# Sixteen-way stores, value loads in two transfers, and the first batch's values summed on VectorE, in a fused attention and expert kernel

## The chip, the cores and the metric

The kernel runs on one core of a Trainium2 chip. The core has TensorE (PE, matrix multiply; its weight loads are listed as PEld), VectorE (DVE), ScalarE (ACT), GpSimd (POOL) and SyncE (SP). DMA moves data between DRAM and the on-chip memory SBUF; here POOL issues the loads, SP and, in the last batch, ACT issue the stores. Matmul results go to a second memory, PSUM, which VectorE and ScalarE read. The metric is the device time of one execution in microseconds (us).

## The reference

Eight batches, eight heads, 576 rows, head size 64. Keys and values are averaged over groups of 8 rows (72 groups), and the attention output of all heads, 4608 rows of 512, goes to a top-1 router over eight experts. Cut to what matters:

```python
k_p = k.reshape(B, H, 72, 8, D).mean(axis=3);  v_p = v.reshape(B, H, 72, 8, D).mean(axis=3)
attn = softmax(q @ k_p.T / sqrt(D));           x = attn @ v_p          # to (4608, 512)
logits = normalize(x) @ normalize(expert_emb).T / tau
e = argmax(logits);  gate = softmax(logits)[e]
out = gate * (relu(x @ w1[e]) @ w2[e])         # w1[e]: 512x1024, w2[e]: 1024x512
```

## The kernel before, in words

The batches are worked on one after another, with the attention of the next batch laid between the expert matmuls of the present one. For each batch the kernel guesses one expert for all of its rows, from the router's logits of the batch's mean row, and loads that expert's weights while the attention still runs. After the last batch it checks the guess; a loop (line 1068, called the repair loop here) would redo rows for other experts. In these data it has nothing to do, but every engine passes its entry, where it waits on the semaphores of everything that is still under way.

**Attention of a batch** (`attention`). POOL loads k, q and v (`load_k`, `load_q`, `load_v`, lines 880 to 900), converting from float32 to float16. v lands as 72 partitions (groups) of 8 heads x 8 rows x 64. VectorE adds key rows in pairs and transposes them (`k0`, `k1`, `kT`), and transposes q in three parts called units (`q0` to `q2`, line 432). For each unit u, TensorE makes scores (line 471), ScalarE takes exp (478), TensorE multiplies by the values (`pv`, 489), VectorE divides by the row sums (`xs`, 499 and 501) and transposes the result into `xt_all` (`x_turn`, 507), which holds x as the later matmuls want it; ScalarE squares it for the norm (`square`, 516). When all three squares are there, `route` (530) makes the logits and the norms.

**Values.** In batches 1 to 7 VectorE adds the eight value rows of a group in three halving steps (`v_add`, 445 and 449), in place, into `vpx`. In batch 0 TensorE sums them as eight matmuls with the identity (`v_sum`, 455), and ScalarE copies the sum into `vpx` (`v_out`, 461). The mean row that the guess needs comes from `vpx` (`mean`, 593), in batch 0 from the raw values (`mean_raw`, 602: 64 matmuls of one column, 8 heads x 8 rows). `guess` (615), `guess_out` with MAX8 (622) and a register load on POOL lead to the issue of the weight loads (319, 324).

**Experts of a batch** (`ffn`). "Hidden" matmuls (`h_part`, 749) make 64 groups of 128 hidden values: two of the eight (w = 0, 1; the argument `early` is 2) in three parts, one for each unit, as soon as that unit's x is there; the other six in halves of 288 columns. ScalarE applies relu (`relu`, 758). "y" matmuls (`y_part`, 769; `y_last`, 798) make four tiles of 128 rows (c = 0 to 3) and one of 64 rows held as two half rows (c = 4). ScalarE or VectorE multiplies by the gate (786, 788, 807) and `store` (877) writes the tile out. The last batch's tile c = 3 is written to `y_end` (780, 782) and stored in two pieces after the repair loop (1113 on SP, 1114 on ACT).

**Rows.** Row i*36 + t of a batch (i of 16, t of 36) stands in column t*16 + i of `xt_all`, so a y tile's partitions are 8 t by 16 i, and a store's outer dimension in DRAM is t: 8 for c < 4, 4 for c = 4 and for each piece of `y_end`.

**What sets the order.** A planner (`Plan`) gives each step an engine, an estimated time, the steps it needs and a priority, tries 400 random shifts of the priorities, and writes the instructions out in the order found. Each engine then runs its list in order and waits on semaphores. Changed estimates or dependencies therefore change the order everywhere. In stretches where the plan has TensorE idle it writes filler matmuls (`warm`, 371), which are fixed in the program. The waits come from the tile framework, which compares which parts of a tile an instruction reads and writes.

Of the kernel before, what the change touches and what calls it, by code (L numbers as in the profile page):

```python
# [242 lines left out]
def kernel(  # L243
# [114 lines left out]


# [26 lines left out]
    def attention(b, early=False):  # L386
# [54 lines left out]
        def v_add(level):  # L441
            vv = loads['v', b].rearrange("g h (r d) -> g h r d", d=D)
            n = POOL >> (level + 1)
            if level < 2:
                nc.vector.tensor_tensor(out=vv[:, :, 0:n], in0=vv[:, :, 0:n],  # L445
                                        in1=vv[:, :, n:2 * n], op=ALU.add)
                return
            new_vpx()
            nc.vector.tensor_tensor(out=st['vpx'][:, :, 0:D], in0=vv[:, :, 0],
                                    in1=vv[:, :, 1], op=ALU.add)  # L450

        def v_sum():
            st['pv'] = psum()
            for r in range(POOL):
                nc.tensor.matmul(out=st['pv'][0:G, 0:H * D], lhsT=ident_h[0:G, 0:G],
                                 rhs=loads['v', b][:, :, ts(r, D)],
                                 start=(r == 0), stop=(r == POOL - 1))

        def v_out():
            new_vpx()  # L460
            nc.scalar.copy(out=st['vpx'][:, :, 0:D],
                           in_=st['pv'][0:G, 0:H * D].rearrange("g (h d) -> g h d", h=H))
# [42 lines left out]
        def x_turn(u):  # L505

            nc.vector.transpose(  # L507
                out=xt_all[:, b].rearrange("p w (t l) -> p t w l", l=32)[:, ts(u, 6)],
                in_=st['x', u].rearrange("p b j d -> p (b j d)").rearrange(
                    "p (t l w) -> p t w l", w=4, l=32))  # L510

        def square(u):
            if 'sq' not in st:
                st['sq'] = xp.tile([128, 4, S], BF16, name="sq", bufs=1)
            cs = ts(u, 192)
            nc.scalar.activation(out=st['sq'][:, :, cs], in_=xt_all[:, b, :, cs],  # L516
                                 func=AF.Square)
# [79 lines left out]
        def mean_raw():  # L597

            pm = st['pm'] = psum()
            for h in range(H):  # L600
                for r in range(POOL):
                    nc.tensor.matmul(out=pm[ts(h % 2, 64), h // 2:h // 2 + 1],
                                     lhsT=loads['v', b][:, h, ts(r, D)], rhs=ones_m[0:G, 0:1],
                                     start=(r == 0), stop=(r == POOL - 1))
# [75 lines left out]
        if early:  # L680
            step('mean', 'PE', 1.5, mean_raw, ['lv', 'const'], -30, tiles=1)
            step('vs', 'PE', 1.75, v_sum, ['lv', 'guess'], -25, tiles=1)
            step('v', 'ACT', 0.5, v_out, ['vs'], -30, frees=[('vs', 0)])
# [20 lines left out]
        for u in range(NU):  # L704
            step(f's{u}', 'PE', 0.53, lambda u=u: score(u),
                 ['kT', f'q{u}', (f'pv{u}', b - 1)], b - 10, tiles=2)
            for p in range(2):
# [6 lines left out]
            step(f'x{u}', 'DVE', 0.92, lambda u=u: x_turn(u), [f'xs{u}'], b - 1.6)  # L714
            step(f'sq{u}', 'ACT', 0.75, lambda u=u: square(u),
                 [f'x{u}', ('route', b - 1)], b - 4)
# [15 lines left out]
    def ffn(plan, b, xt, w, get_gm, finish, last=False, early=0):  # L732
# [9 lines left out]
        def h_part(w, u):  # L742


            n, step_ = (SU, 256) if w < early else (HALF, 512)
            if u == 0:
                st['ph', w] = psum(plan)
            for kk in range(4):
                nc.tensor.matmul(out=st['ph', w][:, ds(u * step_, n)],  # L749
                                 lhsT=w1v[:, kk, w // 4, (w // 2) % 2, w % 2, :],  # L750
                                 rhs=xt()[:, kk, ts(u, n)],
                                 start=(kk == 0), stop=(kk == 3))

        def relu(w):
            n, step_ = (SU, 256) if w < early else (HALF, 512)
            if ('hT', w // 4) not in st:
                st['hT', w // 4] = hp_.tile([128, 2, 2, S], FP16, name=f"hT{w // 4}")
            nc.scalar.activation(  # L758
                out=st['hT', w // 4][:, (w // 2) % 2, w % 2, :].rearrange(
                    "p (r c) -> p r c", c=n),  # L760
                in_=st['ph', w].rearrange("p (r c) -> p r c", c=step_)[:, 0:S // n, 0:n],
                func=AF.Relu)
# [60 lines left out]
        for w, u in order:  # L823
# [3 lines left out]
            hs[w, u] = chain(0.33 if w < early else 0.495, lambda w=w, u=u: h_part(w, u), xs,  # L827
# [13 lines left out]
        for part in parts:  # L841
            if part is None:
                o = chain(0.98, y_last, before('lw2', 'copy') + relus, 1)
                plan.step('ACT', 1.4 if last else 0.85, y_last_out, [o, *gm], -10 + pri,
                          frees=[(o, 0)], store=0.45)
# [5 lines left out]
            if half:  # L851
                o = ys[c if last else c // 2 * 2, 0]
                if last:
                    plan.step('DVE' if c % 2 == 0 else 'ACT', 0.7 if c % 2 == 0 else 1.2,
                              lambda c=c: y_out(c), [ys[c, 1], *gm], -10 + pri,
                              frees=[(o, 0)], store=0.82)
                elif c % 2:
                    for i in (c - 1, c):
                        plan.step('ACT', 0.6, lambda i=i: y_out(i), [ys[i, 1], *gm],
                                  -10 + pri, frees=[(o, 0)] if i == c else [], store=0.82)  # L860
# [3 lines left out]
    def out_rows(o_b, c, y_sb):  # L864

        rows = o_b.rearrange("(i t) d -> t i d", t=T)
        if c < 4:
            return [(rows[ts(c, 8)], y_sb)]
        DH = DM // 2
        return [(rows[32:T, :, ts(j, DH)], y_sb[ts(j, 64), 0:DH]) for j in range(2)]  # L870
# [11 lines left out]
    with tc.manual_schedule():  # L882
# [6 lines left out]
        def load_v(b, after=()):  # L889
            def emit():  # L890
                vv = loads['v', b] = inp.tile([G, H, POOL * D], FP16, name="vv")
                nc.gpsimd.dma_start(out=vv, in_=grouped(v, b))
            done['lv', b] = load(0.9, 3.6, emit, [('v', b - 2), ('vs', b - 2), *after])
# [218 lines left out]
    for dst, src in out_rows(out[ts(B - 1, S)], 3, y_end):  # L1112
        nc.sync.dma_start(out=dst[0:4], in_=src[0:64])
        nc.scalar.dma_start(out=dst[4:8], in_=src[64:128])
# [34 lines left out]
```

The softmax here doesn't subtract the row's maximum and nothing guards it: scores larger than these inputs give would overflow.

## Time and profile before

| | us |
|---|---|
| runs | 219.91, 219.10, 218.87, 215.33 |
| median | 218.99 |
| the profiled execution's own time | 217.82 |
| its span, first to last instruction | 216.1 |
| TensorE busy in the span | 191.1 (88%), of it 17.0 in 58 fillers |
| VectorE, ScalarE, POOL busy | 143.8, 126.4, 35.3 |
| first y matmul of batch 0 | 36.18 |
| compute ends (`y_end` written) | 206.60 |
| last store issued, landed | 211.39, 215.15 |

Busy shares are averages over three stretches that have different limits: the head up to the first y matmul, the middle, and the tail after the last matmul. Busy time of matmuls is modelled from a pipeline; an engine that is busy may still wait a little. Landings are read from the semaphores that a transfer's parts post.

### The profile page before, as it was taken

Reading aid. Unit: us, or ns where it says so; the run is one execution under the profiler, and the core shown is the slowest. Engines: PE = TensorE matmul, PEld = TensorE weight load, DVE = VectorE, ACT = ScalarE, POOL = GpSimd, SP = SyncE. Lnnn points to the kernel's source line nnn. Section 1 sums busy time; section 2 is a strip of 40 time slices with the busy share of each in tenths; the row PEclk is TensorE's granted clock in tenths of the full one; section 3 lists DMA queues with packets and bytes.
Section 4 is the critical chain, followed back from the end, with each engine's and each line's share of the span. In section 5 each row is a group of like instructions: output and inputs, shape, how many; then the busy total and the mean of one; then the engine's idle time right before and its main releaser. Section 6 shows DMA issues by size and latency. Waiting matters only on the chain. (4 is left out here: it accounts for less than half of the span.)

```text
span 216.1 us, 7393 instructions
## 1 busy us (share of the span) xinstructions
PE 191.1 (88%) x3155; PEld 119.9 (56%) x3156; DVE 143.8 (67%) x391; ACT 126.4 (58%) x203; POOL 35.3 (16%) x61
## 2 busy tenths in 40 slices
PE   6879999988987999997998999889998999999900
PEld 2355586455752487455864586448654864586400
DVE  3745968199689836976796869766977895642200
ACT  3037455594693377547766768477857677775300
POOL 7107026003200043003201420132000100020000
PEclk9985699999996999999999999999999999999995
DMA  4998999999997269999984999999955400340231
GB/s 76 192 160 136 207 217 185 208 222 234 251 212 131 46 165 199 208 222 195 243 164 91 194 207 239 212 226 224 239 135 142 167 1 11 92 125 1 55 123 53
DMA packets 18486, 34.63 MB, mean 160 GB/s; under 512 B 2440, under 2 KB 9224, under 8 KB 17936
## 3 DMA queue, kind: packets, MB, share of 16 engines
q0 software_dynamic: 12992, 24.65, 62.3%
q1 hardware_dynamic: 5184, 9.00, 13.0%
q8 instruction: 26, 0.43, 0.8%
q10 hardware_dynamic: 272, 0.46, 0.6%
q14 instruction: 12, 0.10, 0.1%
HBM read 61.88 MB, written 9.44 MB: 330 GB/s over the span
## 5 line engine op out<-in xcount | busy, mean ns | idle before, releaser
L749 PE MATMUL pa<-xt_all,w 128*128 128x288 f16 (+1 forms) x576 | 67.6, 273 | 1.6 <-DVEq L666 0.6
L769 PE MATMUL pa<-w,hT 128*128 128x512 f16 x256 | 62.8, 386 | 4.9 <-ACT y_sb L786 2.8
L749 PEld LDWEIGHTS <-w 128*128 128x128 f16 x576 | 52.3, 98 | 14.7 <-issue 4.2
L758 ACT ACTIVATE hT<-pa 128x576 f16<-128x576 f32 x64 | 40.7, 647 | 17.3 <-PE pa L749 16.5
L478 ACT ACTIVATE at<-pa 72x768 f16<-72x768 f32 x48 | 36.6, 803 | 12.4 <-PE pa L471 12.0
L769 PEld LDWEIGHTS <-hT 128*128 128x128 f16 x256 | 23.4, 98 | 31.4 <-issue 7.5
L786 ACT ACTIVATE y_sb<-pa,gm 128x512 f32<-128x512 f32 x29 | 19.1, 685 | 24.8 <-PE pa L769 24.7
L516 ACT ACTIVATE sq<-xt_all 128x768 bf16<-128x768 f16 x24 | 20.0, 842 | 10.4 <-DVE xt_all L507 10.2
L432 DVE STREAM_TRANSPOSE qT<-qq 128x768 f16<-128x768 f16 x24 | 22.6, 962 | 3.1 <-DMA qq<-in_q_dram 2.9
L501 DVE TENSOR_TENSOR x_sb<-pa,rc 128x768 f16<-128x768 f32 x24 | 23.0, 957 | 0.8
L507 DVE STREAM_TRANSPOSE xt_all<-x_sb 128x768 f16<-128x768 f16 x24 | 22.8, 965 | 0.3
L319 POOL DMA_DIRECT2D w<-in_moe_w_dram x10 | 4.2, 417 | 96.4 <-DMA w<-in_moe_w_dram 40.4
L499 DVE RECIPROCAL rc<-pa 128x12 f32<-128x12 f32 x24 | 5.3, 222 | 21.2 <-PE pa L489 20.7
L547 POOL TENSOR_TENSOR rn<-lgT,half_c 128x5 f32<-128x5 f32 x8 | 9.5, 1190 | 56.5 <-DVE lgT L552 56.5
L371 PE MATMUL pa<-ones_m 128*128 128x512 f16 x58 | 17.0, 437 | 1.7 <-DVE half_c L975 1.7
L489 PEld LDWEIGHTS <-at 72*32 72x32 f16 x1152 | 11.9, 100 | 8.7 <-ACT at L478 4.6
L471 PE MATMUL pa<-qT,kT 32*72 32x192 f16 x384 | 14.3, 257 | 2.4 <-DVE kT L423 0.9
L489 PE MATMUL pa<-vpx,at 72*32 72x65 f16 x1152 | 14.9, 201 | 1.7 <-ACT at L478 1.4
L471 PEld LDWEIGHTS <-kT 32*72 32x72 f16 x384 | 8.5, 111 | 10.8 <-issue 5.5
L445 DVE TENSOR_TENSOR vv<-vv 72x2048 f16<-72x2048 f16 (+1 forms) x14 | 13.1, 935 | 0.2
L552 DVE STREAM_TRANSPOSE lgT<-pa 128x160 f32<-128x160 f32 x8 | 2.8, 349 | 14.5 <-PE pa L530 14.5
L371 PEld LDWEIGHTS <-ones_m 128*128 128x128 f16 x58 | 5.9, 108 | 8.1 <-issue 3.2
(98 smaller groups left out, 151.8 us busy)
## 6 DMA issues: line engine op xcount, KB each, us to landing
w<-in_moe_w_dram POOLq DMA_DIRECT2D x14, 1024.0 KB, 16.3
out_dram<-y_sb SPq DMA_DIRECT2D x30, 256.0 KB
kk<-in_k_dram POOLq DMA_DIRECT2D x8, 576.0 KB, 17.4
vv<-in_v_dram POOLq DMA_DIRECT2D x8, 576.0 KB, 25.3
qq<-in_q_dram POOLq DMA_DIRECT2D x7, 576.0 KB, 17.7
w<-in_moe_w_dram POOLq DMA_DIRECT2D x4, 512.0 KB, 6.5
out_dram<-y_sb SPq DMA_DIRECT2D x15, 64.0 KB
qq<-in_q_dram POOLq DMA_DIRECT2D x1, 384.0 KB
```

The lines of the kernel that those rows point to most:

```text
L371: nc.tensor.matmul(out=pa[:, 0:512], lhsT=ones_m[:, 0:128], rhs=ones_m[:, 0:512], start=True, stop=True)
L432: nc.vector.transpose(out=qT.rearrange("p w r (t i) -> p t w r i", i=16), in_=qq.rearrange("p t (w r i) -> p t w r i", w=2, r=2))
L471: nc.tensor.matmul(out=pS[a // 2][0:G, ds(a % 2 * 512 + r * SU, SU)], lhsT=kT[ts(a, 32), w, r, :], rhs=qT[ts(a, 32), w, r, :], start=(w == ...
L478: nc.scalar.activation(out=at.rearrange("g a r c -> g a (r c)"), func=AF.Exp, scale=escale, in_=st['pS', u][p][0:G].rearrange("g (a c) -> ...
L489: nc.tensor.matmul(out=px[ts(a, 32), c0:c0 + D + 1], lhsT=st['at', u, a // 2][:, a % 2, r, ts(j, 32)], rhs=st['vpx'][:, 2 * a + r, 0:D + 1 ...
L501: nc.vector.tensor_tensor(out=x_sb, in0=pxv[:, :, :, 0:D], in1=rc.unsqueeze(3).to_broadcast([128, 2, 6, D]), op=ALU.mult)
L507: nc.vector.transpose(out=xt_all[:, b].rearrange("p w (t l) -> p t w l", l=32)[:, ts(u, 6)], in_=st['x', u].rearrange("p b j d -> p (b j d ...
L516: nc.scalar.activation(out=st['sq'][:, :, cs], in_=xt_all[:, b, :, cs], func=AF.Square)
L749: nc.tensor.matmul(out=st['ph', w][:, ds(u * step_, n)], lhsT=w1v[:, kk, w // 4, (w // 2) % 2, w % 2, :], rhs=xt()[:, kk, ts(u, n)], start ...
L758: nc.scalar.activation(out=st['hT', w // 4][:, (w // 2) % 2, w % 2, :].rearrange("p (r c) -> p r c", c=n), in_=st['ph', w].rearrange("p (r ...
L769: nc.tensor.matmul(out=py, lhsT=st['hT', w // 4][:, (w // 2) % 2, w % 2, ts(c, 128)], rhs=w2[:, w // 2, w % 2, :], start=(w == 0), stop=(w ...
L786: nc.scalar.activation(out=y_sb, in_=py, func=AF.Copy, scale=g)
```

## The change

- **Stores.** The columns of `xt_all` are laid out so that a y tile's partitions are 16 i by 8 t (c = 4: 16 i by 4 t), and a store's outer dimension in DRAM is 16. For this the transpose of a unit writes single columns 8 apart (4 apart in the last 64 columns) and is made in two pieces of four and two blocks of 32, since a unit's six blocks fall into two column tiles. `y_end` is stored in two column halves instead of two row halves.
- **Units of columns.** Finished columns after units 0, 1 and 2 are now 0 to 128, to 384 and to 576; the squares and the hidden matmuls of w = 0, 1 go by these thirds (`third`). The square of a unit is declared to need all transposes up to its own.
- **Value loads.** Each goes in two transfers, of 64 and of 8 partitions.
- **Batch 0's values.** `v_sum` and `v_out` go; `v_add` sums on VectorE, into a tile of the pool that later holds hidden values, since `mean_raw` still reads the raw values. `mean_raw` takes heads in pairs, whose outputs lie in different halves of the columns.
- **The planner** gets other estimates for transposes, squares, hidden parts, value loads and stores.

```diff
+    def third(u):
+        return slice((0, 128, 384)[u], (128, 384, S)[u])
...
         def v_add(level):
             vv = loads['v', b].rearrange("g h (r d) -> g h r d", d=D)
             n = POOL >> (level + 1)
+            to = vv
+            if early:
+                if level == 0:
+                    half = hp_.tile([128, 2, 2, S], FP16, name="hT0")
+                    st['half'] = half[0:G].rearrange("g a r s -> g (a r s)")[
+                        :, 0:H * 4 * D].rearrange("g (h r d) -> g h r d", h=H, d=D)
+                to = st['half']
+                if level > 0:
+                    vv = to
             if level < 2:
-                nc.vector.tensor_tensor(out=vv[:, :, 0:n], in0=vv[:, :, 0:n],
+                nc.vector.tensor_tensor(out=to[:, :, 0:n], in0=vv[:, :, 0:n],
...
         def x_turn(u):
-            nc.vector.transpose(
-                out=xt_all[:, b].rearrange("p w (t l) -> p t w l", l=32)[:, ts(u, 6)],
-                in_=st['x', u].rearrange("p b j d -> p (b j d)").rearrange(
-                    "p (t l w) -> p t w l", w=4, l=32))
+            src = st['x', u].rearrange("p b j d -> p (b j d)").rearrange(
+                "p (m s i w) -> p m w s i", w=4, s=2, i=16)
+            m = 0
+            for c, n in ((0, 4), (1, 2), (1, 2), (2, 4), (3, 4), (4, 2))[2 * u:2 * u + 2]:
+                m0 = 2 if (c, u) == (1, 1) else 0
+                nc.vector.transpose(
+                    out=xt_all[:, b, :, cols(c)].rearrange(
+                        "p w (i m s) -> p m w s i", i=16, s=2)[:, m0:m0 + n],
+                    in_=src[:, m:m + n])
+                m += n
         def square(u):
-            cs = ts(u, 192)
+            cs = third(u)
...
         def mean_raw():
-            for h in range(H):
+            for h in range(0, H, 2):
                 for r in range(POOL):
-                    nc.tensor.matmul(out=pm[ts(h % 2, 64), h // 2:h // 2 + 1],
-                                     lhsT=loads['v', b][:, h, ts(r, D)], rhs=ones_m[0:G, 0:1],
+                    for i in range(2):
+                        nc.tensor.matmul(out=pm[ts(i, 64), h // 2:h // 2 + 1],
+                                         lhsT=loads['v', b][:, h + i, ts(r, D)],
...
         if early:
             step('mean', 'PE', 1.5, mean_raw, ['lv', 'const'], -30, tiles=1)
-            step('vs', 'PE', 1.75, v_sum, ['lv', 'guess'], -25, tiles=1)
-            step('v', 'ACT', 0.5, v_out, ['vs'], -30, frees=[('vs', 0)])
+            step('v0', 'DVE', 0.85, lambda: v_add(0), ['lv'], -25)
+            step('v', 'DVE', 0.9, lambda: [v_add(1), v_add(2)], ['v0'], -25)
...
-            step(f'x{u}', 'DVE', 0.92, lambda u=u: x_turn(u), [f'xs{u}'], b - 1.6)
-            step(f'sq{u}', 'ACT', 0.75, lambda u=u: square(u),
-                 [f'x{u}', ('route', b - 1)], b - 4)
+            step(f'x{u}', 'DVE', 0.98, lambda u=u: x_turn(u), [f'xs{u}'], b - 1.6)
+            step(f'sq{u}', 'ACT', (0.54, 0.96, 0.75)[u], lambda u=u: square(u),
+                 [*(f'x{i}' for i in range(u + 1)), ('route', b - 1)], b - 4)
...
         def h_part(w, u):
-            n, step_ = (SU, 256) if w < early else (HALF, 512)
+            cs = third(u) if w < early else slice(u * HALF, u * HALF + HALF)
+            to = cs.start + 128 if w < early else u * 512
...
     def out_rows(o_b, c, y_sb):
-        rows = o_b.rearrange("(i t) d -> t i d", t=T)
+        rows = o_b.rearrange("(i t) d -> i t d", t=T)
         if c < 4:
-            return [(rows[ts(c, 8)], y_sb)]
+            return [(rows[:, ts(c, 8)], y_sb)]
         DH = DM // 2
-        return [(rows[32:T, :, ts(j, DH)], y_sb[ts(j, 64), 0:DH]) for j in range(2)]
+        return [(rows[:, 32:T, ts(j, DH)], y_sb[ts(j, 64), 0:DH]) for j in range(2)]
...
                 vv = loads['v', b] = inp.tile([G, H, POOL * D], FP16, name="vv")
-                nc.gpsimd.dma_start(out=vv, in_=grouped(v, b))
-            done['lv', b] = load(0.9, 3.6, emit, [('v', b - 2), ('vs', b - 2), *after])
+                for gs in (slice(0, 64), slice(64, G)):
+                    nc.gpsimd.dma_start(out=vv[gs], in_=grouped(v, b)[gs])
+            done['lv', b] = load(1.4, 3.1, emit, [('v', b - 2), ('mean', b - 2), *after])
...
     for dst, src in out_rows(out[ts(B - 1, S)], 3, y_end):
-        nc.sync.dma_start(out=dst[0:4], in_=src[0:64])
-        nc.scalar.dma_start(out=dst[4:8], in_=src[64:128])
+        for eng, cs in ((nc.sync, slice(0, DM // 2)), (nc.scalar, slice(DM // 2, DM))):
+            eng.dma_start(out=dst[:, :, cs], in_=src[:, cs])
```

## The prediction

> **What bounds the kernel now.** I read the page first, then the waits of TensorE, then the head and the tail as timelines, because the busy shares say that the middle is full and the ends are not.
>
> ```profile
> PE 191.1 (88%) x3155; PEld 119.9 (56%) x3156; DVE 143.8 (67%) x391; ACT 126.4 (58%) x203; POOL 35.3 (16%) x61
> PEclk9985699999996999999999999999999999999995
> ```
>
> TensorE is busy 88% of the span, 17.0 us of it with 58 fillers (L371). The second line is its granted clock in 40 slices of 5.4 us: about half speed in slices 4 and 5, lower in slice 13. Its waits from 24 to 206 us:
>
> ```profile
> PE pa L769 <- ACT y_sb L786: 2.8, 6, 0.7
> PE pa L769 <- issue: 2.1, 2, 1.2
> PE pa L489 <- ACT at L478: 0.9, 3, 0.4
> ```
>
> They are small and scattered, and no load stands among the large ones: in the middle it is TensorE's own work, in the planner's order, that sets the time. The head, in time order (start, duration, then the instruction):
>
> ```profile
> 12.45 1.49 PE L602 MATMUL pa<-ones_m,vv 72*64 72x1 f16 x64 [0.85 <-DMA vv<-in_v_dram]
> 13.91 0.98 DVE L432 STREAM_TRANSPOSE qT<-qq 128x768 f16<-128x768 f16 x1 [2.90 <-DMA qq<-in_q_dram]
> 14.41 2.99 PE L455 MATMUL pa<-vv,ident_h 72*72 72x512 f16 x8
> 17.44 0.58 ACT L461 CAST vpx<-pa 72x512 f16<-72x512 f32 x1 [3.31 <-PE pa L455]
> 22.16 2.74 PE L371 MATMUL pa<-ones_m 128*128 128x512 f16 x6
> 27.07 1.15 PE L749 MATMUL pa<-xt_all,w 128*128 128x192 f16 x12
> 36.18 4.48 PE L769 MATMUL pa<-w,hT 128*128 128x512 f16 x20
> ```
>
> The value sum takes TensorE 2.99 us at half clock (granted 0.50 from 15.07 to 25.3 us), and the first y matmul comes at 36.18. The tail, and DMA from 203 to 216 us in 40 slices of 0.33 us (busy tenths, GB/s):
>
> ```profile
> 206.13 0.47 ACT L782 ACTIVATE y_end<-pa,gm 128x256 f32<-128x256 f32 x1 [2.86 <-DVE y_end L780]
> 210.23 1.07 ACTq L1114 DMA_DIRECT2D out_dram<-y_end  x1
> 211.39 0.59 SPq L1113 DMA_DIRECT2D out_dram<-y_end  x1
> DMA  2552354554457564411000000131222222210000
> GB/s 82 142 66 32 57 158 158 183 176 164 176 202 246 189 208 170 164 69 76 32 0 0 0 0 25 50 57 38 63 101 101 95 76 101 101 69 6 0 0 0
> ```
>
> Compute ends at 206.6; the last stores are issued 3.6 and 4.8 us later. Between lie the repair loop's semaphore waits (L1068). The trace's semaphore events say which binds: SP has passed seven of them by 207.4, passes the c=1 store's at 208.30 and the c=2 store's at 209.89, the moment those stores land. The last store, started at 212.36, lands at 215.15. So **the path's last 9.5 us are stores**.
>
> **Stores on sixteen engines.** How many DMA engines a transfer uses can be counted in the semaphore events: of 16 posts, the engines left out post at once. A c<4 store (outer dimension 8) has eight late posts, a 64 KB store (outer 4) four. After the change the outer dimension is 16 everywhere. Rows for the price: four engines with 16 KB each land 1.4 to 1.6 us after the first post (201.79 to 203.38); eight with 32 KB each, queue empty, 2.5 to 3.4 (189.30 to 192.70); overlapped, 4.2 (c=2, 205.70 to 209.87). With sixteen, c=2 is 16 KB per engine: 1.5 us, landing at 207.2, ahead of the waits SP walks through anyway. SP then passes at 207.6 instead of 209.89: 2.3 us. The end store goes from 32 KB on each of four engines (2.8 us) to 8 KB on each of sixteen: I take 1.5, gaining 1.3. Sum 3.6. Lower bound: sixteen engines together reach no more than the 200 GB/s that eight show above; then c=2's 256 KB take 1.3 us plus the 0.9 that the 64 KB row leaves over (1.6 less 64 KB at half that rate), landing at 207.9, and the end stores' 256 KB take 2.2; the gains are 1.9 and 0.6: 2.5. Upper: the end store in 1.2, so 3.9. I take **3.6**. Earlier stores need no price: no row shows TensorE waiting for one.
>
> **Value loads in two transfers.** The first load shows four posts at 8.12 to 8.38 and twelve at 11.57 to 12.40: twelve engines, six rows each. After: 64 rows are four per engine, the other eight add one on eight engines, so five rows instead of six; 4.3 us from 8.06 becomes 3.6, landing near 11.7 instead of 12.40. POOL issues one more transfer per load; its issue rows (L892 0.87, L899 0.56) put that at about 0.5 us, eight times, under a POOL that is 16% busy. Not shown is an 8-row load; its issue lies between nothing, since it cannot shorten the first one's, and one L892 more.
> The Trainium skill ("DMA: Bandwidth & Descriptors", Rules for kernel authors) advises against two transfers to disjoint partitions, as both spread over the same engines anyway. The same page (Why a DMA increments its semaphore by 16 and not by 1) takes the largest count up to 16 that divides the outer sizes, 12 for 72 rows, and the twelve late posts agree. By the first rule the load gains nothing, by the second 0.7 us; the total moves by neither, as follows.
>
> **Batch 0's values on VectorE.** TensorE loses eight matmuls (2.99) and ScalarE one cast (0.58); VectorE gets three adds. Batch 1's same adds run from 25.18 to 27.53: 2.35 us. They stand ahead of the second q transpose, so 11.75 to 14.1, then q until 15.0, and the expert choice (MAX8, 14.81 before) comes 0.15 later: the first weights are issued at 16.65 instead of 16.50. The raw mean with alternating column tiles is 64 matmuls; bounds are 1.49 (no gain) and 1.2 (the already alternating mean, L593, eight in 0.29); it ends before the adds either way and hides. The mean now precedes the first score (11.07 before, about 13.0 after); its exp ends at 15.0 and nothing waits longer for it than for the second q.
> So P·V no longer waits for 18.02: second score 15.0 to 15.9, P·V 0 to 16.7, two fillers, third score at 17.6, its exps until 20.2, P·V 2 ends at 21.1 instead of 22.2. But the planner puts nine fillers there (six before), fixed in the program: at half clock 9 x 0.427 = 3.85, until 24.9.
>
> **New waits.** The changed kernel's built instructions show what the diff does not: the second transpose piece of unit 1 now waits for unit 0's square, the first piece of unit 2 for unit 1's square and, in batches 0, 1 and 3, for hidden matmuls (L749) of unit 1. Before, transposes waited for VectorE alone. In batch 0, after the fillers, unit 0's eight matmuls end near 25.7, w=0 of unit 1 at 26.2 to 26.6, and only then does the transpose run (0.95): hidden matmuls of unit 2 start at 27.3 to 27.7. Before, at 27.07, 16 remained; now 8. From there: 8 x 0.088 + 48 x 0.1225 + route, mean and guess 1.2 = 7.8, five fillers 1.1: first y matmul at 36.2 to 36.6 against 36.18. **Head: +0.2.** Behind the waiting transpose stand batch 1's value adds (27.3 instead of 25.18), its guess and the next weights' issue (32.84), covered by DMA work queued until 39.8. Clock bounds: full speed again at 21.9 saves 1.9; half speed until 28.7 costs 1.7.
> In the other batches unit 2's scaling (0.23 + 0.96, start to start about 1.2) stands before the wait, and the 4 x 256 square needs about 1.05 (768 elements take 0.84): hidden, 0. Cover gone, about 1 us a batch.
>
> **Two pieces per transpose.** 24 more instructions at 0.06 (0.86 start to start against 0.80 of elements at the rate of L414 and L432): 1.4 us of VectorE at 67%. No row shows a transpose writing every eighth element; L423's scattered 128 elements cost 0.085 us more than its 32, under 1 ns an element, so I take no loss; the other end is twice 0.86, some 20 us of VectorE. Hidden matmuls in 128/256/192 instead of 3 x 192: columns unchanged, 0.
> **Middle.** Fillers are again 58 and waits look alike; I take 0, between -2.9 and +2.9, the price of one stall with clock drop (1.2 us at 65 to 66.4, then 3.4 at half speed: 1.7).
>
> **Sum.** -3.6 + 0.2 = -3.4: 217.82, the profiled execution, becomes 214.4. The median before, 218.99, lies 1.2 above that execution; part of that should recur, so I say **215.2**.
>
> **Rivals.**
> 1. Forecast, tail gain and an even rest: 213 to 217.5. 0.50.
> 2. Head or middle also gains, since fillers run at full clock or the 65 us stall goes: 215.2 - 1.9 to 2.9, so 212.5. For it: P·V 2 is 1.1 us earlier. Against: nothing in the trace ties the return of the clock at 25.3 to one instruction. 0.23.
> 3. The stores do not spread or the loop still waits for their landing: tail 0 to -1, 218.5. Against it: the counts 8 and 4 above. 0.11.
> 4. Slower: ScalarE, in order, reaches unit 1's square late, the transposes stall VectorE and hidden matmuls follow. It decides once the square ends more than 1.2 us after unit 1's transpose; at 1 us in eight batches, 8 - 3.4: 223.5. For it: waits the planner does not know. Against: ScalarE 58% busy. 0.16.
>
> A measurement of this kernel tells about 2% (4.4 us) from no change. Case 1 lies on both sides of 214.6, a third of it below; with case 2 faster is 0.40. Same takes the rest of 1, case 3 and a quarter of 4: 0.48. Slower 0.12. The range leaves out case 4's far half and the best tenth: 211.5 to 220.
>
> **What would show it.** Store semaphores with no early posts; the final SP store about 2.5 us after y_end instead of 4.8, landing within 1.7; twelve late posts gone from the value loads; VectorE busy up by 3 to 4 us; a first y matmul at 36 to 37. Wrong if transposes take over 0.6 us for 512 elements, VectorE idles on ACT L525 ahead of L515, or TensorE's clock drops more often than once after 30 us.

## The result and the profile after

The changed kernel takes **266.7 us** (median of 10 runs, 260.95 to 267.56) against 218.13 us for the kernel before (15 runs). Some executions of either kernel are in a slower state, which ratios and differences in this document leave out and medians do not: without it the two take 262.5 (three runs) and 217.1 us, ratio **1.209, 95% interval 1.198 to 1.220**. The forecast was 215.2. The kernel is slower by 45 us, on the other side and far outside the range.

The profiled execution has a span of 260.8 us at a mean granted TensorE clock of 0.896 (0.953 before). The engines' busy times and the granted clock in 40 slices of 6.5 us, from the page of the changed kernel:

```profile
PE 200.8 (77%) x3147; PEld 125.1 (48%) x3148; DVE 203.0 (78%) x418; ACT 125.3 (48%) x202; POOL 38.9 (15%) x69
PEclk9965779985999797997799988999999958999997
```

VectorE has 59 us more than before (143.8) and TensorE's share is down from 88% to 77%. The clock now dips all along the span instead of twice. The groups by line and tile show where VectorE's time comes from (busy us, mean ns of one, idle time before it):

```profile
L515 DVE STREAM_TRANSPOSE xt_all<-x_sb 128x512 f16<-128x512 f16 x24 | 60.5, 2522 | 3.6 <-PE pa L761 2.7
L515 DVE STREAM_TRANSPOSE xt_all<-x_sb 128x256 f16<-128x256 f16 x24 | 30.2, 1256 | 0.2
```

These are the two pieces of each transpose of x (`x_turn`). In the kernel before it is one instruction a unit:

```profile
L507 DVE STREAM_TRANSPOSE xt_all<-x_sb 128x768 f16<-128x768 f16 x24 | 22.8, 965 | 0.3
```

One of 768 elements took 0.965 us, 22.8 us in all; now a unit takes 3.0 to 3.65 us, and the page counts 81.8 us for the line (the records of two pieces overlap). The waits (us in total, times, longest) show who pays:

```profile
PEld L761 <- issue: 36.8, 26, 5.6
ACT sq L525 <- DVE xt_all L515: 35.4, 14, 5.1
PE pa L761 <- DVE xt_all L515: 19.3, 7, 5.4
DVE xt_all L515 <- PE pa L761: 2.7, 2, 1.7
```

The first line is idle time of the hidden matmuls' weight loads, for which the profile names no releaser; the squares (L525) wait 35.4 us for transposes, and the hidden matmuls themselves (L761) up to 5.4 us at a time, where the longest wait of TensorE in the middle had been about 1.2. The last line is one of the prediction's new waits, a transpose held up by a hidden matmul: it is there, and small. A transpose that waits for a square (L525), which the fourth rival needed, does not show here. The head, as a timeline (start, duration, instruction):

```profile
12.80 1.22 DVE L459 TENSOR_TENSOR hT<-vv 72x2048 f16<-72x2048 f16 x1 [0.89 <-DMA vv<-in_v_dram]
12.85 1.18 PE L612 MATMUL pa<-ones_m,vv 72*64 72x1 f16 x64 [2.79 <-DMA vv<-in_v_dram]
19.10 3.65 DVE L515 STREAM_TRANSPOSE xt_all<-x_sb 128x512 f16<-128x512 f16 x2
23.81 3.58 DVE L515 STREAM_TRANSPOSE xt_all<-x_sb 128x256 f16<-128x256 f16 x2
28.54 3.00 DVE L515 STREAM_TRANSPOSE xt_all<-x_sb 128x512 f16<-128x512 f16 x2
43.30 4.48 PE L782 MATMUL pa<-w,hT 128*128 128x512 f16 x20
```

Values arrive no earlier than before; the three transposes take 10.2 us of the head, and the first y matmul comes at 43.30 instead of 36.18. The tail:

```profile
254.12 0.47 ACT L795 ACTIVATE y_end<-pa,gm 128x256 f32<-128x256 f32 x1 [3.29 <-DVE y_end L793]
256.32 0.57 ACTq L1128 DMA_DIRECT2D out_dram<-y_end  x1
257.39 0.56 SPq L1128 DMA_DIRECT2D out_dram<-y_end  x1
```

Here the change does what was forecast: from `y_end` written (254.59) to the end of the span 6.18 us pass, before 9.50.

### The profile page after: what moved, and what is told of

It is laid out like the page before. It is cut to its first block, busy times and chain, and to the rows that moved or that the text cites. A ratio compares the mean times of both kernels' runs of the same rounds, so it can differ in the third digit from the quotient of the medians.

```text
span 260.8 us, 7425 instructions
## 1 busy us (share of the span) xinstructions
PE 200.8 (77%) x3147; PEld 125.1 (48%) x3148; DVE 203.0 (78%) x418; ACT 125.3 (48%) x202; POOL 38.9 (15%) x69
## 5 line engine op out<-in xcount | busy, mean ns | idle before, releaser
L761 PE MATMUL pa<-xt_all,w 128*128 128x288 f16 (+3 forms) x576 | 79.2, 295 | 33.3 <-DVE xt_all L515 19.3
L515 DVE STREAM_TRANSPOSE xt_all<-x_sb 128x512 f16<-128x512 f16 (+1 forms) x48 | 81.8, 1889 | 3.9 <-PE pa L761 2.7
L761 PEld LDWEIGHTS <-w 128*128 128x128 f16 x576 | 56.3, 106 | 51.3 <-issue 36.8
L782 PE MATMUL pa<-w,hT 128*128 128x512 f16 x256 | 60.4, 386 | 1.0 <-ACT y_sb L799 0.8
L525 ACT ACTIVATE sq<-xt_all 128x512 bf16<-128x512 f16 (+2 forms) x24 | 20.2, 843 | 56.6 <-DVE xt_all L515 35.4
L782 PEld LDWEIGHTS <-hT 128*128 128x128 f16 x256 | 24.2, 99 | 29.1 <-issue 3.0
L799 ACT ACTIVATE y_sb<-pa,gm 128x512 f32<-128x512 f32 x29 | 19.1, 680 | 13.3 <-PE pa L782 11.7
L375 PE MATMUL pa<-ones_m 128*128 128x512 f16 x58 | 20.1, 498 | 1.7 <-DVE half_c L989 1.7
L501 DVE RECIPROCAL rc<-pa 128x12 f32<-128x12 f32 x24 | 6.4, 267 | 8.1 <-PE pa L491 7.3
L375 PEld LDWEIGHTS <-ones_m 128*128 128x128 f16 x58 | 6.5, 120 | 9.5 <-issue 5.2
```

Of the source, the lines that this page charges most:

```text
L375: nc.tensor.matmul(out=pa[:, 0:512], lhsT=ones_m[:, 0:128], rhs=ones_m[:, 0:512], start=True, stop=True)
L515: nc.vector.transpose(out=xt_all[:, b, :, cols(c)].rearrange("p w (i m s) -> p m w s i", i=16, s=2)[:, m0:m0 + n], in_=src[:, m:m + n])
L761: nc.tensor.matmul(out=st['ph', w][:, ds(to, cs.stop - cs.start)], lhsT=w1v[:, kk, w // 4, (w // 2) % 2, w % 2, :], rhs=xt()[:, kk, cs], s ...
L782: nc.tensor.matmul(out=py, lhsT=st['hT', w // 4][:, (w // 2) % 2, w % 2, ts(c, 128)], rhs=w2[:, w // 2, w % 2, :], start=(w == 0), stop=(w ...
L799: nc.scalar.activation(out=y_sb, in_=py, func=AF.Copy, scale=g)
```

## The experiments

The theory is that single results written 8 elements apart make the transposes slow, and that this alone makes the loss. The rivals are the new waits, the planner's order on estimates that were too low, and the head.

### Contiguous writes, all else as changed

```diff
                     out=xt_all[:, b, :, cols(c)].rearrange(
-                        "p w (i m s) -> p m w s i", i=16, s=2)[:, m0:m0 + n],
+                        "p w (m s i) -> p m w s i", i=16, s=2)[:, m0:m0 + n],
```

> The changed kernel with one thing altered: a transpose writes each block of 32 results as one contiguous run again, into the same columns, still in two pieces per unit, with the same steps, estimates and order on every engine. The rows of a tile are then stored in another order than the reference has (rows exchanged inside a tile, the same work). Theory 1, the scattered writes alone make the loss: 128x512 takes 0.55 to 0.60 us instead of 2.52, 128x256 about 0.30 instead of 1.26, VectorE's busy time falls from 203 to about 146 us, and the time falls to 213 to 218 us, which was the forecast for the whole change. Theory 2, the new waits of transposes on squares and hidden matmuls, or the planner's new order, make it: the transposes get cheap, but the time stays above 235 us. Both in part: between 218 and 235.

Measured: **215.13 us** against 218.03, ratio 0.988 (0.981 to 0.995). The engines' busy times, from the page of this run:

```profile
PE 192.9 (90%) x3147; PEld 121.5 (57%) x3148; DVE 148.7 (70%) x418; ACT 125.1 (59%) x202; POOL 39.0 (18%) x69
```

and its transposes of x, from the groups:

```profile
L515 DVE STREAM_TRANSPOSE xt_all<-x_sb 128x512 f16<-128x512 f16 x24 | 16.7, 696 | 0.5
L515 DVE STREAM_TRANSPOSE xt_all<-x_sb 128x256 f16<-128x256 f16 x24 | 10.0, 416 | 0.2
```

VectorE is back at 70%, and the pieces take 0.70 and 0.42 us (0.55 to 0.60 and about 0.30 had been expected). The steps stand in the changed kernel's order on every engine. One string takes 47.4 us away (262.5 to 215.1), and what is left of the change comes out near what the forecast gave to the whole. One caution belongs to it: with contiguous writes the framework also finds no overlap between transposes and earlier reads, so the new waits go too. The pairs below separate the two.

### Half of the batches

```diff
-                        "p w (i m s) -> p m w s i", i=16, s=2)[:, m0:m0 + n],
+                        "p w (i m s) -> p m w s i" if b > 3 else
+                        "p w (m s i) -> p m w s i", i=16, s=2)[:, m0:m0 + n],
```

> The changed kernel with scattered writes in batches 4 to 7 alone, contiguous runs in batches 0 to 3 (rows exchanged inside the tiles of batches 0 to 3, the same work). Theory 1 with every batch bound by VectorE's chain in the same way: half of the loss, 240 us, 3 either way, and the lost time lies behind 120 us of the trace. If the loss were set by the first batches, where nothing covers the transposes (head), it would be nearly all gone: under 230. Theory 2, waits and order: no change, above 255.

Measured: 237.81 us, ratio 1.091 (1.083 to 1.100), 22.7 us above the run with contiguous writes for 27.4 us more VectorE time (176.1). The first y matmul of batch 3 comes at 114.8 (113.4 with contiguous writes), that of batch 4, whose transposes are slow, at 144.5 (137.1), and the last tile is written at 230.3 (207.9). The loss lies in the batches whose transposes scatter: these four batches, far from the head, make 22.7 of the 47.4 us.

### Prices of writes

The kernel before, with extra instructions over 512 fp16 elements ahead of its work, for instance:

```diff
+            for n in (1, 2, 4, 8):
+                nc.vector.transpose(out=far[:, 0:512 * n].rearrange("p (a n) -> p a n", n=n)[:, :, 0],
+                                    in_=src)
```

> The kernel before with a row of extra VectorE and ScalarE instructions ahead of its first work, all over 512 fp16 elements per partition, written into a region that is written over later: transposes whose results lie 1, 2, 4 and 8 elements apart; the old form and the changed kernel's form; runs of 2, 4, 8 and 16 results with gaps between them; and plain copies to results 1 and 8 apart on both engines. Only the rows' durations matter, the time is longer by design. Theory A, every result that does not follow the one before costs a full access of its own: 2, 4 and 8 apart all cost the same, about 2.1 us against 0.55, and runs of r cost about 2.1/r plus 0.5. Theory B, the distance sets it: 2 apart near 0.6 to 1.1, 4 apart near 1.8 (the changed kernel's 256 results 4 apart took 0.93, 8 apart 1.31 to 1.54), 8 apart the most. On plain copies: if the cost belongs to the transposing alone, 8 apart costs the same as 1 apart.

Measured, from the timeline of VectorE: results 1, 2, 4 and 8 apart; the old form with a spaced read (L983); the changed form (L985); runs of 2 with 16 from one run to the next (L988):

```profile
1.66 0.71 DVE L981 STREAM_TRANSPOSE xt_all<-ones_m 128x512 f16<-128x512 f16 x1
2.41 0.75 DVE L981 STREAM_TRANSPOSE xt_all<-ones_m 128x512 f16<-128x512 f16 x1
3.20 1.32 DVE L981 STREAM_TRANSPOSE xt_all<-ones_m 128x512 f16<-128x512 f16 x1
4.55 2.46 DVE L981 STREAM_TRANSPOSE xt_all<-ones_m 128x512 f16<-128x512 f16 x1
7.04 0.71 DVE L983 STREAM_TRANSPOSE xt_all<-ones_m 128x512 f16<-128x512 f16 x1
7.79 2.46 DVE L985 STREAM_TRANSPOSE xt_all<-ones_m 128x512 f16<-128x512 f16 x1
10.28 0.71 DVE L988 STREAM_TRANSPOSE xt_all<-ones_m 128x512 f16<-128x512 f16 x1
```

The changed form costs exactly what single results 8 apart cost. Distance sets it, theory B; a spaced read is free, and runs of 2 already cost nothing, nor do runs of 4, 8 and 16 (0.71 each). It is no matter of transposing alone: a plain copy goes from 0.29 to 1.31 us on VectorE and from 0.62 to 2.47 us on ScalarE when its results lie 8 apart.

### VectorE's time without scattered writes

```diff
-                nc.vector.transpose(
+                for _ in range(4):
+                    nc.vector.transpose(
```

> The run with contiguous writes, with each transpose of x issued four times over (the same result each time): 4 x (0.63 + 0.33) = 3.8 us a unit, near the 3.65, 3.58 and 3.0 us of the scattered form, without any scattered write. Theory 1, only VectorE's time matters: VectorE busy near 205 to 215 us, time 262 to 275. Rival, scattered writes hold up other engines in the memory: the time stays well below, under 250, though VectorE is as busy.

Measured: 291.55 us, ratio 1.348 (1.335 to 1.361), VectorE busy 230.9. Both are above what was expected: a repeat of a 512 piece takes 0.75 us from start to start, where the other piece follows it after 0.63 in the run with contiguous writes. Against that run 82.2 us more VectorE time cost 76.4 us, 0.93 for one; the scattered writes cost 47.4 us for 54.3, 0.87 for one. So time on VectorE suffices to explain the loss. Nor does ScalarE show a disturbance by the writes: its relu takes 0.649 us in the changed kernel and with contiguous writes, its exp 0.800 and 0.801.

### The planner told the true price

```diff
-            step(f'x{u}', 'DVE', 0.98, lambda u=u: x_turn(u), [f'xs{u}'], b - 1.6)
+            step(f'x{u}', 'DVE', (3.5, 3.5, 2.9)[u], lambda u=u: x_turn(u), [f'xs{u}'], b - 1.6)
```

> The changed kernel with the planner told what its transposes cost: 3.5, 3.5 and 2.9 us a unit instead of 0.98; nothing else. Theory 1, the price itself makes the loss (VectorE's 203 us exceed what the rest leaves it): 250 to 268. Rival, the order planned on an estimate of 0.98 makes it, and a plan with the true price hides most: under 240.

Measured: 254.75 us, ratio 1.178 (1.164 to 1.192), within the range of theory 1. Of the 47.4 us some 8 were the order's, planned on 0.98 us (its two runs lie 3.3 us apart); the other 40 the plan chosen from 400 tries did not hide.

### Pairs, with the right order of rows

If the q transpose puts neighbouring t side by side (its own results 2 apart), the x transpose can keep them together:

```diff
-                out=qT.rearrange("p w r (t i) -> p t w r i", i=16),
-                in_=qq.rearrange("p t (w r i) -> p t w r i", w=2, r=2))
+                out=qT.rearrange("p w r (m i s) -> p m s w r i", i=16, s=2),
+                in_=qq.rearrange("p (m s) (w r i) -> p m s w r i", s=2, w=2, r=2))
...
-                        "p w (i m s) -> p m w s i", i=16, s=2)[:, m0:m0 + n],
+                        "p w (i m s) -> p m w i s", i=16, s=2)[:, m0:m0 + n],
```

> The changed kernel with its layout and row order, but each transpose of x writes pairs of neighbours (runs of 2, 8 elements from one to the next) instead of single elements. For that the q transpose writes its results 2 elements apart, so that two neighbouring t of one i stand side by side. By the price table: 2 apart costs q 0.75 instead of 0.71 us for 512, so about 1.03 instead of 0.97 for 768, 1.5 us of VectorE in all, and runs of 2 cost nothing: x pieces at 0.70 and 0.41 us, as with contiguous runs. Then the time is that of the run with contiguous writes, 215.1, plus at most 0.7: 214.5 to 216. Rival: the table's runs of 2 stood 16 elements apart, and 8 apart they cost as single ones do: pieces at 1.3 to 2.5 us and 235 to 267 us.

Measured: 217.14 us against 217.09, ratio 1.005 (1.001 to 1.009). The pieces take 0.699 and 0.417 us and q 0.999, all as priced, so pairs 8 apart are free. But 214.5 to 216 had been expected, and the time is 0.9% above that of contiguous writes, by the ratios 1.7%. (The kernel before was timed anew with each group of runs and lay between 216.3 and 218.0, so ratios from different groups carry that difference.) The waits of this run:

```profile
ACT sq L525 <- DVE xt_all L515: 12.9, 8, 4.5
DVE xt_all L515 <- PE pa L761: 5.4, 3, 3.4
PE pa L761 <- DVE xt_all L515: 2.0, 3, 1.1
```

The middle line is the wait of a transpose for hidden matmuls of the unit before, 5.4 us in three places; with contiguous writes it does not occur. In the same order of steps, the first y matmuls of batches 0 to 3 come 0.5, 1.1, 1.9 and 2.2 us later than with contiguous writes, and after that the distance stays at 1.9 to 2.2. The three waits stand in batches 0, 1 and 3, those for which the prediction had named them. But not all of the delay arises there: 0.8 of the 2.2 us comes in batch 2, where a transpose waits 0.6 us for a square.

### Two ways around the waits

```diff
-                        *(f'x{i}' for i in range(u + 1 if w < early else u + 2)))
+                        *(f'x{i}' for i in range((1, 3, 3)[u] if w < early else u + 2)))
```

> The run with pairs, with the hidden matmuls of unit 1 (w = 0, 1) declared to need unit 2's transposes too, so that no transpose of a batch can be made to wait for hidden matmuls of unit 1; some waits for squares and for unit 0's matmuls are left. The run with pairs came 2.2 us later to the last matmul than the one with contiguous runs (210.1 against 207.9), all of it gained in batches 0, 1 and 3, where its third transposes waited for those matmuls (5.4 us of VectorE, 3 waits). Theory 1, these waits are the 2.2 us: 215.0 to 216.0, and VectorE's idle time before its transposes falls from 6.8 us to under 3. Rival, the difference is the plan's or the clock's: 216.5 to 218.

Measured: 217.31 against 217.98, ratio 0.998 (0.994 to 1.002). VectorE's idle time before its transposes falls from 6.8 to 2.6 us, as expected, but the last tile is written at 210.4, where the run with pairs had 210.1. The planner had found another order, which takes 28.0 us between the first y matmuls of batches 3 and 4, where the run with pairs took 23.5. The theory's forecast of 215 to 216 missed.

```diff
-            for c, n in ((0, 4), (1, 2), (1, 2), (2, 4), (3, 4), (4, 2))[2 * u:2 * u + 2]:
...
+            for m in (0, 2, 4):
+                c, m0 = divmod(6 * u + m, 4)
```

> The run with pairs, with each unit's transpose in three pieces of two blocks instead of one of four and one of two; this changes which parts of the tile the framework takes for overlapping. The waits on squares in unit 1 go, those of unit 2 on matmuls of unit 1 in batches 0, 1 and 3 stay; a unit's transposes take 3 x 0.36 instead of 0.63 + 0.40. Theory 1, the waits on matmuls of unit 1 cost the 2.2 us: no change against the run with pairs, 216.5 to 218. Rival, the waits on squares cost them: 215 to 216.

Measured: 216.85, ratio 0.996 (0.992 to 0.999): within theory 1's range, with the wait for hidden matmuls left at 4.8 us, and 0.1% below the run with pairs in time (0.9% by the ratios). So the 2.2 us of the new waits, of both kinds, rest on the pair of runs with one order (contiguous against pairs, which also differ by 0.9 us of q transposes over all batches); taking the waits for hidden matmuls away by a new plan did not confirm them.

### The head's parts alone

The kernel before with the two-part value loads, `v_add` in batch 0 and the interleaved raw mean; for instance:

```diff
-                nc.gpsimd.dma_start(out=vv, in_=grouped(v, b))
+                for gs in (slice(0, 64), slice(64, G)):
+                    nc.gpsimd.dma_start(out=vv[gs], in_=grouped(v, b)[gs])
```

> The kernel before with only these parts of the change: value loads in two transfers, batch 0's values summed on VectorE into the spare tile, raw mean with two column tiles interleaved; transposes, units of columns and stores are those of before. By the prediction's step for the head: +0.2 us, first y matmul within 0.5 us of 36.18, time 217 to 219.5. Rival, the head gains what TensorE loses of the value sum (2.99 us): 215 to 216. Rival, values arrive no earlier in two transfers and VectorE's adds delay the second q transpose and the guess by 1.2 us (as MAX8 at 16.02 instead of 14.81 in the changed kernel suggests): 219 to 221.

Measured: 218.44 against 218.03, ratio 0.996 (0.989 to 1.002): no difference, as the prediction's step has it. In the profiled execution, which took 219.27 us, the first y matmul comes at 35.4 instead of 36.2, and that of batch 1 at 66.4 instead of 64.8.

### The head's parts undone

Three versions with cheap transposes (late hidden matmuls, pairs, three pieces), each with the diff above turned round, for instance:

```diff
-            step('v0', 'DVE', 0.85, lambda: v_add(0), ['lv'], -25)
-            step('v', 'DVE', 0.9, lambda: [v_add(1), v_add(2)], ['v0'], -25)
+            step('vs', 'PE', 1.75, v_sum, ['lv', 'guess'], -25, tiles=1)
+            step('v', 'ACT', 0.5, v_out, ['vs'], -30, frees=[('vs', 0)])
```

> As the run with the late hidden matmuls of unit 1, but with the value loads in one transfer, the value sum of batch 0 on TensorE and the raw mean as in the kernel before: what is left of the change is the layout with pairs, the units of columns and the stores. By the run of the head's parts alone (no difference to the kernel before): within 1 us of the run that has them, 214.5 to 216.5. Rival, the head's parts cost what the last matmul came later with contiguous runs (207.9 against 206.6 before): 213 to 214.5.

Measured: **214.48 us against 217.98, ratio 0.982 (0.977 to 0.987)**. The end of its timeline:

```profile
206.81 0.47 ACT L795 ACTIVATE y_end<-pa,gm 128x256 f32<-128x256 f32 x1 [3.29 <-DVE y_end L793]
208.70 0.56 ACTq L1127 DMA_DIRECT2D out_dram<-y_end  x1
209.63 0.56 SPq L1127 DMA_DIRECT2D out_dram<-y_end  x1
```

The last tile is written at 207.28, 0.7 us later than in the kernel before, and the span ends at 212.86, 3.2 us earlier: the tail's gain with nearly nothing lost ahead of it. This version beats both kernels, with the rows in the right order. That the head's parts make no difference (within 1 us of the run that has them) missed: it is 2.8 us faster without them, at the upper end of the rival's range.

> The run with pairs, with the value loads, batch 0's value sum and the raw mean as in the kernel before (the head's parts of the change undone); hidden matmuls of unit 1 as in the change. Theory 1, the head's parts cost some 2.8 us wherever the transposes are cheap, as the two runs with late hidden matmuls say (217.3 with them, 214.5 without): 214 to 215 against 217.1 with them. Rival, the 2.8 us were the luck of one plan, and the head's parts cost nothing, as alone on the kernel before (ratio 0.996): 216.5 to 218.

Measured: 216.21 against 219.66, ratio 0.992 (0.985 to 0.999); the runs that the ratio uses average 215.5 and 217.2. That lies between the two theories.

> The run with three pieces of two blocks, with the head's parts undone in the same way. Theory 1: 213.5 to 215 against 216.9 with them. Rival: 216 to 218. If the two runs without the head's parts disagree by over 2 us, the plan's order decides, and no price can be given to the head's parts from single plans.

Measured: 215.05 against 219.66, ratio 0.991 (0.983 to 0.999); the runs that the ratio uses average 215.1 and 217.2. All three versions are faster without the head's parts, by the ratios 1.5, 1.3 and 0.5%, by the average times of the same runs 1.5, 0.8 and 0.9%; the last two are near the noise. But the first y matmul is not earlier without them (37.3, 38.1 and 37.6 against 35.9, 37.5 and 37.4), so it is not the head's own time; with them the planner's order of all that follows is another. How much of it is a price of these parts and how much is one plan's order stays open.

### Order chosen in the scores

```diff
-                            lhsT=kT[ts(a, 32), w, r, :], rhs=qT[ts(a, 32), w, r, :],
+                            lhsT=kT[ts(a, 32), w, r, :],
+                            rhs=qT[ts(a, 32), w, r, :].rearrange(
+                                "p (m t i) -> p m i t", m=3, t=4),
```

> The kernel before with another way to stores on sixteen engines and nothing else: the score matmul reads its 192 q columns in another order (16 i, 4 t, in three groups of 64; neighbours in the read 16 elements apart), so that all later work is as before, transposes contiguous in one piece, and each store of 128 rows becomes two of 64 rows with an outer dimension of 16. Theory 1, TensorE streams spaced columns at no loss: score matmuls stay at 0.257 us, and the tail's gain alone remains: 214 to 216. Rival, spaced reads cost TensorE as spaced writes cost VectorE: score matmuls at 0.5 us and more, 384 of them, at 88% busy: over 240.

Measured: 232.55 against 217.09, ratio 1.073 (1.065 to 1.081). The score matmuls of this run:

```profile
L471 PE MATMUL pa<-qT,kT 32*72 32x192 f16 x384 | 38.3, 502 | 1.1 <-ACT hT L760 0.6 <-DVE kT L423 0.3
```

(A store of 128 rows is two of 64 here.) The score matmuls take 0.502 instead of 0.257 us and 24 us more in all. The rival's direction is right, its 240 us were too much; the tail gained as elsewhere.

### More prices

The same place as in the first table, with other distances, copies and matmuls (`apart(n)` is a view with results n elements apart):

```diff
+            for n in (3, 5, 6, 7, 9, 12, 16):
+                nc.vector.transpose(out=apart(n)[:, :, 0], in_=src)
...
+            for n in (1, 2, 4, 8, 16):
+                for _ in range(8):
+                    nc.tensor.matmul(out=pa[:, 0:512], lhsT=ones_m[:, 0:128],
+                                     rhs=apart(n)[:, :, 0], start=True, stop=True)
```

> The kernel before with another row of extra instructions ahead of its first work, into a region that is written over later. VectorE transposes of 512 with results 3, 5, 6, 7, 9, 12 and 16 apart and pairs 4 and 8 apart; copies of 512 on VectorE and ScalarE to results 2, 4 and 16 apart and from sources 8 apart; matmuls whose 512 streamed columns stand 1, 2, 4, 8 and 16 apart, and weight loads of 128 columns 1, 2 and 8 apart. Theory A, distance decides, up to some distance: 3 apart between 0.75 and 1.32 us, 5 to 7 between 1.32 and 2.46, 9 and more at 2.46 or higher. Theory B, powers of two decide (results that fall on the same bank): 3, 5, 7 and 9 near 0.71, 12 as 4 and 16 above 2.46. Pairs 0.71 in both. Streams: the score matmuls with columns 16 apart took 0.50 instead of 0.26 us; by A the loss begins at some smaller distance and grows, or it is one step of two.

Measured, from VectorE's timeline: results 3, 6, 9 and 16 apart, then pairs 8 apart:

```profile
11.28 1.04 DVE L985 STREAM_TRANSPOSE xt_all<-ones_m 128x512 f16<-128x512 f16 x1
13.99 1.90 DVE L985 STREAM_TRANSPOSE xt_all<-ones_m 128x512 f16<-128x512 f16 x1
18.14 2.43 DVE L985 STREAM_TRANSPOSE xt_all<-ones_m 128x512 f16<-128x512 f16 x1
23.06 2.31 DVE L985 STREAM_TRANSPOSE xt_all<-ones_m 128x512 f16<-128x512 f16 x1
26.15 0.71 DVE L987 STREAM_TRANSPOSE xt_all<-ones_m 128x512 f16<-128x512 f16 x1
```

Theory A in the main: the price rises with each element of distance, and powers of two play no part. From 8 on it is flat or falls a little, where 2.46 or more had been expected.

## Why the prediction was wrong, point by point

**Two pieces per transpose: the step that failed.** It said "L423's scattered 128 elements cost 0.085 us more than its 32, under 1 ns an element, so I take no loss", with "twice 0.86, some 20 us of VectorE" as the other end. Both ends were wrong. The rows that it went by, from the kernel before:

```profile
L423 DVE TENSOR_TENSOR kT<-k 128x128 f16<-128x128 f16 x16 | 6.1, 382 | 0.3
L423 DVE TENSOR_TENSOR kT<-k 128x32 f16<-128x32 f16 x8 | 2.4, 297 | 0.0
```

They are read rightly, but do not fit: L423 writes its 128 results in runs of four neighbours (`kTv` in `k_turn`), and for transposes runs of two and more cost nothing (0.71 us); the rows say nothing of single results. In the changed kernel a unit costs 3.0 to 3.65 us instead of 0.965, three to four times. The line's busy time rises by 59 us (81.8 against 22.8), three times the other end. The test that the prediction set itself (over 0.6 us for 512 elements) was met at once with 2.52, and so was its third sign of being wrong: after 30 us the clock falls to half six times before the tail, once in the kernel before. What 24 more instructions cost by themselves was sized about right: with contiguous writes two pieces take 1.04 us together against 0.965 for one, some 1.8 us in all (1.4 forecast).

**Why VectorE at 67% gave no cover.** The prediction let VectorE's share stand for room, but a unit's scaling, transpose, square and hidden matmuls hang on one another, and the next unit's scaling stands behind the transpose on VectorE. So 0.83 to 0.92 us of time follow each us of VectorE (22.7 us for 27.4 when four batches scatter, 24.7 for 26.9 from there to all eight). Part of it shows as a lower clock: TensorE is busy 7.9 us longer than with contiguous writes for the same instructions, at a granted clock of 0.896 against 0.937.

**Stores: right.** 3.6 us were forecast; from `y_end` written to the end of the span it is 3.3 less in the changed kernel and 3.8 with contiguous writes (5.74 against 9.50). All sixteen parts of a store now post late, and SP's last store starts 2.8 us after `y_end` (2.5 forecast, 4.8 before). Its landing takes 2.30 us from the issue, 3.76 before: 1.46 less, where 1.3 was forecast. Counted from the issue the forecast bound of 1.7 was too low; the prediction's 2.8 and 1.5 us count from a store's first post, 0.97 us after the issue, and with all parts posting late that mark is missing.

**Value loads: nothing gained.** The posts spread over sixteen parts as forecast, but the last come at 12.55 and 12.71, where 11.7 was forecast and 12.40 stood before. No run has the loads alone; with the other head parts the total does not move.

**Head: +0.2.** With contiguous writes the first y matmul comes 0.8 us later than before, alone the head's parts make no difference, and their effect within later plans is open.

**New waits.** They are where the prediction put them, and it gave them 0 in the middle. With cheap transposes they go with 2.2 us between two kernels of one order, part of it in batch 2; in the changed kernel they hardly show (2.7 us), where squares and hidden matmuls wait for the transposes anyway. The fourth rival had the right sign (0.12 stood on slower), but its mechanism, VectorE held up by a late square, and its 8 us were not what happened.

**The sum.** Without the failed term it nearly holds: 215.2 was forecast, and the change with contiguous writes, whose rows stand in another order than the reference's, measures 215.13. That the two agree so closely is luck. The forecast took 3.8 us off a median of 218.99; by the ratio the gain is 2.6 us, 3.8 in the tail less 1.3 by which the last tile is written later (207.91 against 206.60), where the forecast had 0.2.

## What to carry to other kernels

A new layout has to be priced by what the writing engine does: look at how many bytes lie side by side in its innermost run. Here single 2-byte results 8 apart cost VectorE and ScalarE 3.5 to 4.5 times as much as neighbours, and pairs cost VectorE's transposes nothing (ScalarE was not tried), so choose an order upstream that keeps two neighbours together. A row from the trace is a price only if its access pattern is the same, run length included. And a busy share of 67% was no cover here: nearly all of the time added to an instruction in the chain that TensorE waits for came out in the total.

## What the runs showed of the hardware

For 512 fp16 results a transpose takes 0.71, 0.75, 1.04, 1.32, 1.60, 1.90, 2.18 and 2.46 us at 1 to 8 elements from one result to the next, and 2.43, 2.42 and 2.31 us at 9, 12 and 16: from 2 to 8 about 0.28 us for each element of distance. Pairs 4, 8 and 16 apart take 0.71 us, and reading 4 apart costs nothing. Copies go the same way at 2, 4, 8 and 16 apart: 0.45, 0.73, 1.31, 1.24 us on VectorE (0.29 side by side), 0.76, 1.32, 2.47, 2.33 us on ScalarE (0.62). Read from a source 8 apart, they take 0.62 and 1.10 us.

The Trainium skill ("SBUF — State Buffer", Specifications (TRN2)) says that the memory has lines of 16 bytes and that each access that crosses to a new line pays; this is the rule that spoke against the change, and the prediction did not weigh it. The flat price from 8 elements (16 bytes) on agrees with it. So do the free pairs, since it asks for two accesses in a line. That 4 apart, also two in a line, cost 1.32 us does not follow from it.

At a granted clock of 0.50 TensorE streams 512 columns that lie 2 elements apart as fast as neighbours (0.427 us from start to start); once the clock has risen, 2 apart take 0.226, and the y matmuls of the kernel before, with neighbours, 0.216. 4 apart it takes 0.451 us and 8 apart 0.900 at a clock of 1.0, and 8 apart stays at 0.900 when the clock falls to 0.50; 16 apart is 0.918 at 0.50. At 8 apart the spacing, not the clock, sets the pace. Weight loads of 128 columns do not slow their matmuls at 1, 2 or 8 apart (0.107 us each, at 0.50).
